# Attention products of a linear-attention and mixture-of-experts kernel in column tiles of 64 queries, with the state update and the zeroing of the output at other places

## The chip, the cores and the metric

The kernel runs on one core of one Trainium2 chip. The metric is the device time of one execution in microseconds (us). Engines are named as the profile names them: PE is TensorE's matmul, PEld its weight load, DVE is VectorE, ACT is ScalarE, POOL is GpSimd, and SP is SyncE, which here only issues transfers (DMAs).

## The reference

Two stages, one after the other. The first is a linear attention with a decaying state, for 4 batches, 8 heads, 768 steps and a head width of 48:

```python
for t in range(S):
    kt, vt, rt = (k[:, :, t], v[:, :, t], r[:, :, t])
    cur = np.einsum('bhd,bhe->bhde', u[None] * kt, vt)
    y[:, :, t] = np.einsum('bhd,bhde->bhe', rt, state + cur)
    state = w[None, :, :, None] * state + np.einsum('bhd,bhe->bhde', kt, vt)
```

The second takes the result as 3072 tokens of 384 numbers and sends each to the two best of 8 experts. A token's noisy logits are `x @ w_gate + log1p(exp(x @ w_noise)) * noise`; the two largest are chosen and weighted by a softmax over the two; an expert is `relu(x @ w1[e]) @ w2[e]` with a hidden width of 1024; the two weighted results are added. All is float32.

## The kernel before, in words

**Attention** goes over 24 tiles i (`NT`): 6 chunks of 128 steps, and in each chunk the 4 batches, so that tile i is chunk `c = i // 4` of batch `b = i % 4`. A tile has 128 queries on the partitions, and its 8 heads stand as 4 pairs `p` with two heads `s` each. Decay is folded into the keys and queries by powers of `w`, so that a chunk needs three products: the scores of keys against queries, masked to the past; the masked scores times the values; and the queries times the state left by the chunk before.

The order of the work is written out by hand, in the loop at L978. Every engine goes through its own instructions in that order, and waits only on semaphores. Iteration i of the loop puts on the engines, one after the other:

- `load(i+3)` (L117): three DMAs from SP for k, r and v of a later tile, in packets of one head's 48 numbers. SP also issues the store of `x` and the loads of expert weights, in the same queue; from tile 8 on, `out` is zeroed there in 16 pieces of 192 rows (L983), since the experts later add into it.
- `trans(i+1)` (L336): keys and queries of the next tile are transposed on PE (L340), and come out of PSUM through ACT (`kT`, L343) and DVE (`rT`, L345).
- `xtrans(i-1)` (L417): the last tile's result transposed on PE (L420), copied by ACT (L422). `zup(i-1)` (L373): the new state, on DVE (`zt`, L381) and ACT (`z` L383, `zb` L385).
- `uterm_b(i+1)`, `prep_k(i+2)`, `uterm_a(i+2)`: the `u` term and decayed keys on POOL (L313 to L322), DVE (L327, and L330 up to tile 8) and ACT (`cv` L333, later).
- `yout(i)` (L388): for each pair one product of the queries with the state (L394, 96 columns wide, from chunk 1 on) and two products of masked scores `AM` with values (L402), all into one PSUM bank `py`. The values are 48 wide, but each product streams them twice, the second time into 48 columns of the bank that nobody reads. Stationary is in both cases a 128x128 block with all 128 queries.
- `xout(i)` (L406): DVE adds the `u` term (L410) and SP stores the result.
- `logits(i-1)` (L425): 3 products with the gate and noise weights (L432); the 16 columns are streamed `LREP` = 6 times side by side, and one copy is read.
- `scores(i+1)` (L348): 8 products with 64 rows each (L352), and `mask(i+1)` (L356): two DVE operations (L360) that write `AM` of the next tile.
- `kvup(i)` (L364): 8 products of keys and values for the next state (L370), 48 columns each, into partitions 0 to 47 and 64 to 111 of the bank `pwarm`. None in the last chunk.

PE makes two passes, each with its own weight load, of every float32 product, so 8 products are x16 in the profile. Between these steps `rstep(us)` (L945) puts pieces of the routing of the tiles 0 to 7, and later 8 to 15, on DVE: each call may spend some us of credit (1.2, 1.1 and 0.3 in a tile), and it holds still for two calls around each of the few PE pieces of the routing.

**Experts** follow. `xT` transposes gathered tokens and splits them into a high and a low part; `p1` makes the hidden layer (L863) and `p2` the output (L897), with three products for each full one. The first products of expert 0, `p1(0, 0)`, begin at about 164 us. The routing of the last 8 tiles goes on beside them, and scatters into `out` follow when the gates are known.

Of the kernel before, what the change touches and what calls it, by code (L numbers as in the profile page):

```python
# [34 lines left out]
NLD = 4  # L35
XT_AT_0 = 4
XT_AT = 4
LREP = 6
NOT = 4

W_LD = {1: (0,), 2: (1, 2), 4: (3,), 5: (4,), 6: (5,), 7: (6,)}
# [5 lines left out]
def kernel(  # L47
# [14 lines left out]
    nc = tc.nc  # L62
    B, H, S, D = r.shape
    N, E = noise.shape
    DM = H * D
# [4 lines left out]
    ND = DM // 128  # L70
    NF = FF // 128
    NT = B * NCH
# [42 lines left out]
    rt, kt, vt = {}, {}, {}  # L115
# [21 lines left out]
    wg = const.tile([128, ND, 2 * E], F32, name="wg")  # L137
# [48 lines left out]
    kT, rT = {}, {}  # L186
# [43 lines left out]
    zrow = const.tile([128, DM], F32, name="zrow")  # L230
# [133 lines left out]
    def kvup(i):  # L364
        c, b = divmod(i, B)
        if c == NCH - 1:
            return
        for p in range(NP):
            for s in range(2):
                nc.tensor.matmul(kvp[s * 64:s * 64 + D, p, :], kd[i % 3][:, 2 * p + s, :D],  # L370
                                 vt[i][:, 2 * p + s, :], start=True, stop=True)
# [16 lines left out]
    def yout(i):  # L388
        c, b = divmod(i, B)
        pyb = psum.tile([128, 512], F32, name="py", tag="py0")  # L390
        py = pyb[:, :DM].rearrange("p (h d) -> p h d", d=D)
        for p in range(NP):
            if c:
                nc.tensor.matmul(py[:, 2 * p:2 * p + 2, :], rT[i][:, p, :], ZB[b][:, p, :],  # L394
                                 start=p == 0, stop=False, skip_group_check=True)
            for s in range(2):


                h = 2 * p + s
                o1 = pyb[:, h * D:(h + 1) * D]  # L400
                o2 = bass.AP(tensor=o1.tensor, offset=o1.offset, ap=[o1.ap[0], [DM - h * D, 2], [1, D]])
                nc.tensor.matmul(o2, AM[i][:, s, p, :], vt[i][:, h, None, :].to_broadcast([128, 2, D]),  # L402
                                 start=not c and h == 0, stop=h == H - 1, skip_group_check=True)
        PY[i] = py

    def xout(i):  # L406
# [8 lines left out]
    XT = {}  # L415
# [9 lines left out]
    def logits(i):  # L425
        g = [i >= a for a, _ in GROUPS].count(True) - 1
        j = i - GROUPS[g][0]
        if j == 0:
            LG[g] = att_pool[0].tile([128, GB, 2 * E], F32, name="lg")
        pl = psum.tile([128, LREP, 2 * E], F32, name="pl", tag="py1")  # L430
        for d in range(ND):
            nc.tensor.matmul(pl, XT[i][:, d, :], wg[:, d, None, :].to_broadcast([128, LREP, 2 * E]),  # L432
                             start=(d == 0), stop=(d == ND - 1))
        nc.scalar.activation(LG[g][:, j, :], pl[:, 0, :], AF.Copy)


# [410 lines left out]
    def p1(e, ci):  # L847
        w_ = sum(tw(t) for t in chunks(e)[ci])
        xh, xl = XH[e, ci]
        wh, wl = W[e][0]  # L850
        wb = w_ // 128 * 128
        hb = moe.tile([128, NF, 2, 3 * 128], F32R, name="hb", bufs=1)
        ht = moe.tile([128, NF, 2, TAIL], F32R, name="ht", bufs=1) if w_ > wb else None
        HH[e, ci] = (hb, ht)
        parts = [(hb[:, :, :, :wb], 0, wb)] + ([(ht, wb, w_)] if w_ > wb else [])
        for f in range(NF):
            fs = slice(f * 128, (f + 1) * 128)
            nph[0] += 1
            ph = (psum.tile([128, WMAX], F32, name="ph", tag="pa", bufs=2) if nph[0] % 3 else
                  psum.tile([128, WMAX], F32, name="ph", tag="kv"))  # L860
            q = [(a, x, d) for d in range(ND) for a, x in ((wh, xh), (wh, xl), (wl, xh))]
            for j, (a, x, d) in enumerate(q):
                nc.tensor.matmul(ph[:, :w_], a[:, d, fs], x[:, d, :w_], start=(j == 0), stop=(j == len(q) - 1))  # L863
            for h_, a, b in parts:
                nc.scalar.activation(h_[:, f, 0, :], ph[:, a:b], AF.Relu)  # L865
            for h_, a, b in parts:
                nc.vector.scalar_tensor_tensor(h_[:, f, 1, :], ph[:, a:b], 0.0, h_[:, f, 0, :].bitcast(F32),  # L867
                                               op0=ALU.max, op1=ALU.subtract)
            yield
# [3 lines left out]
    def p2(e, ci, step=None):  # L873
        hb, ht = HH[e, ci]
        wh, wl = W[e][1]
        offs = {t: 128 * j for j, t in enumerate(chunks(e)[ci])}

        ts = chunks(e)[ci]
        for t in ts if (e, ci) != seq[-1] else ts[-1:] + ts[:-1]:
            n, o = tw(t), offs[t]  # L880
            py = psum.tile([128, DM], F32, name="pym", tag=f"py{np2[0] % 2}")
            np2[0] += 1
            ot = moe.tile([128, DM], F32, name="ot", bufs=NOT)
            OT[e, t] = ot
            hs = slice(o, o + n)
            if n == 64:
                for f in range(NF):
                    nc.tensor.matmul(py, ht[:, f].rearrange("p a b -> p (a b)"), wh[:, f, :], start=(f == 0), stop=(f == NF - 1),  # L888
                                     skip_group_check=True)
                    nc.tensor.matmul(py[:n], ht[:, f, 0, :], wl[:, f, :], start=False, stop=(f == NF - 1),  # L890
                                     skip_group_check=True)
                nc.scalar.activation(ot[:n], py[64:], AF.Copy)
                nc.vector.tensor_add(ot[:n], py[:n], ot[:n])
            else:
                q = [(a, x, f) for f in range(NF) for a, x in ((0, wh), (0, wl), (1, wh))]
                for j, (a, x, f) in enumerate(q):
                    nc.tensor.matmul(py, hb[:, f, a, hs], x[:, f, :], start=(j == 0), stop=(j == len(q) - 1))  # L897
                    if step and j % 8 == 7:
                        step()
                if (e, ci) == seq[-1]:  # L900
                    OT[e, t] = py
                else:
                    nc.scalar.activation(ot, py, AF.Copy)  # L903
            yield t
# [40 lines left out]
    def rstep(us):  # L945

        credit[0] = min(credit[0] + us, 1.6 * us + 0.2)
        while route_q:
            if at_pe[0] > 0:
                at_pe[0] -= 1  # L950
                if at_pe[0] > 0:
                    return
            if credit[0] <= 0:
                return
            try:
                c = next(route_q[0])
            except StopIteration:
                route_q.pop(0)
                continue
            if c == "pe":  # L960
                at_pe[0] = gap[0]
                credit[0] -= 0.3
                return
            credit[0] -= c or 0.2
# [6 lines left out]
    def route_when_done(i):  # L971
        for g, (a, b) in enumerate(GROUPS):
            if b == i + 1:
                if not route_q:
                    at_pe[0] = gap[0]
                route_q.append(route(g))

    for i in range(NT):  # L978
        if i + NLD - 1 < NT and i + NLD - 1 > 2:
            load(i + NLD - 1)  # L980
        if i >= NT - 16:
            q = (i - NT + 16) * 192
            nc.sync.dma_start(out[q:q + 192, :].rearrange("(p two) d -> p two d", two=2),  # L983
                              zrow[:96, None, :].to_broadcast([96, 2, DM]))
        if i + 1 < NT:
            trans(i + 1)
        if i == 0:
            prep_k(0, nc.vector)
            uterm_b(0)
        if i:  # L990
            xtrans(i - 1)
            zup(i - 1)
        if i == I_EARLY:
            while GEARLY - 1 not in routed:
                rstep(1)
            early()
        if i + 1 < NT:
            uterm_b(i + 1)
        if i + 2 < NT:
            prep_k(i + 2)  # L1000
            uterm_a(i + 2)
        for p in W_HI.get(i, ()):
            next(wun[p])
        rstep(STEPS_A)
        if i == 0:
            flag = consts_c()
        if i in (0, 3):
            next(flag)
        yout(i)
        xout(i)  # L1010
        if i:
            logits(i - 1)
            route_when_done(i - 1)
        rstep(STEPS_B)
        if i == NT - 1:
            for _ in xT(0, 0):
                pass
            p1a = p1(0, 0)
        if i + 1 < NT:
            scores(i + 1)  # L1020
            mask(i + 1)
        kvup(i)
        rstep(STEPS_KV)
        for p in W_LO.get(i, ()) + W_LD.get(i, ()):
            next(wun[p])
# [4 lines left out]
    next(wun[6])  # L1030
    NLAG[0] = 3
    for j, _ in enumerate(p1a):
        if j == XT_AT_0:
            for _ in xT(0, 1):
                pass
        rstep(STEPS_P1)
    for t in p2(0, 0, lambda: rstep(STEPS_P2 / 3)):
        hold.append((0, t))
    def routes_done():
# [159 lines left out]
```

## Time and profile before

| | |
|---|---|
| time of 3 runs, median | 651.19 us (649.28 to 652.44) |
| span of the profiled execution | 648.8 us |
| mean granted TensorE clock in it | 0.989 |
| PE busy | 625.8 us (96%) |
| PEld busy | 594.9 us (92%) |
| DVE busy | 345.3 us (53%) |
| ACT busy | 262.5 us (40%) |
| POOL busy | 263.2 us (41%) |
| chain that ended last, PE's share | 69% |

The times are of executions without the profiler; the span is from the first to the last instruction of one profiled execution. Shares over the whole span mix the attention, which ends at about 164 us, with the experts, which have a different mix of work, so each is read by itself. [...]

### The profile page before, as it was taken

The numbers are of one execution on the slowest core, as the hardware profiler recorded it, in microseconds if no ns is written. First come the engines' busy times: TensorE is split into PE (matmuls) and PEld (weight loads), VectorE is DVE, ScalarE is ACT, GpSimd is POOL, SyncE is SP. The second block draws the span as 40 slices with busy tenths as digits, with TensorE's granted clock in tenths as the row PEclk, the third lists the DMA queues.
The fourth block names the chain that finished last, engine by engine and source line by source line (L and its number), as shares of the span: only waits on it lengthen the run. The fifth ranks groups of instructions, "written<-read, shape, count | busy, mean of one in ns | idle before, by whom it ended". The sixth has DMA issues, their size and how long they took to land.

```text
span 648.8 us, 11891 instructions
## 1 busy us (share of the span) xinstructions
PE 625.8 (96%) x4436; PEld 594.9 (92%) x4437; DVE 345.3 (53%) x882; ACT 262.5 (40%) x738; POOL 263.2 (41%) x389
## 2 busy tenths in 40 slices
PE   8999999999998988999999999999999999999993
PEld 5899899998998988999999999999999999999993
DVE  6776988786789654436253444525342543523230
ACT  2557667674324244425242433524243342423210
POOL 7857546562012246415422641443273145315211
PEclk9999999999998989999999999999999999999997
DMA  8999877764033256242441624244252425202100
GB/s 129 213 202 198 192 176 168 170 167 114 14 112 117 63 182 199 82 146 94 134 145 71 189 75 153 70 158 140 75 177 75 153 60 178 81 27 87 37 10 30
DMA packets 111444, 78.87 MB, mean 122 GB/s; under 512 B 86721, under 2 KB 101441, under 8 KB 111378
## 3 DMA queue, kind: packets, MB, share of 16 engines
q1 hardware_dynamic: 101442, 49.19, 30.5%
q0 software_dynamic: 9936, 28.83, 14.1%
q8 instruction: 37, 0.61, 0.4%
q14 instruction: 29, 0.24, 0.1%
HBM read 59.03 MB, written 19.76 MB: 121 GB/s over the span
## 4 chain that ended last, share of the span: by engine, by line
PE 69%; DVE 3%; DMA 1%; ACT 1%; issue 0%; POOL 0%; POOLq 0%
PE ph L863 33%; PE pym L897 30%; PE ptm L838 2%; PE pym L890 2%; PE pym L888 2%; DMA stg<-in_moe_w_dram 1%; DVE xl L840 0%; DVE w1l L287 0%; DVE r_oa L516 0%; PE py L402 0%; ACT hb L865 0%; DVE hb L867 0%; PE pl L432 0%; PE RT L529 0%; DVE w0l L287 0%
## 5 line engine op out<-in xcount | busy, mean ns | idle before, releaser
L897 PE MATMUL pym<-w1h,hb 128*128 128x384 f32 x768 | 204.2, 339 | 0.0
L863 PE MATMUL ph<-xh,w0h 128*128 128x384 f32 (+3 forms) x408 | 142.9, 350 | 4.9 <-ACT xh L839 2.8
L918 POOL DMA_INDIRECT out_dram<-ot,TK x56 | 57.2, 1022 | 220.9 <-DVE ot L914 198.1
L863 PE MATMUL ph<-xl,w0h 128*128 128x384 f32 (+3 forms) x408 | 140.1, 343 | 1.8 <-DVE xl L840 1.8
L897 PEld LDWEIGHTS pym<-w1h,hb 128*128 128x128 f32 x768 | 139.4, 188 | 0.8 <-DVE hb L867 0.2
L863 PE MATMUL ph<-xh,w0l 128*128 128x384 f32 (+3 forms) x408 | 140.0, 343 | 0.0
L897 PE MATMUL pym<-w1l,hb 128*128 128x384 f32 x384 | 129.3, 337 | 0.0
L867 DVE SCALAR_TENSOR_TENSOR hb<-ph,hb 128x384 fp32r<-128x384 f32 (+1 forms) x136 | 72.3, 532 | 106.2 <-ACT ht L865 70.1
L865 ACT ACTIVATE hb<-ph 128x384 fp32r<-128x384 f32 (+1 forms) x136 | 64.2, 473 | 118.3 <-PE ph L863 116.0
L903 ACT ACTIVATE ot<-pym 128x384 f32<-128x384 f32 x45 | 22.1, 492 | 160.0 <-PE pym L897 160.0
L863 PEld LDWEIGHTS ph<-xh,w0h 128*128 128x128 f32 x408 | 77.5, 190 | 8.4 <-ACT xh L839 3.4
L811 POOL DMA_INDIRECT xg<-xd,GR x56 | 54.3, 970 | 75.1 <-DVE f L693 32.7
L863 PEld LDWEIGHTS ph<-xl,w0h 128*128 128x128 f32 x408 | 77.8, 191 | 5.0 <-DVE xl L840 2.5
L863 PEld LDWEIGHTS ph<-xh,w0l 128*128 128x128 f32 x408 | 77.6, 190 | 2.6
L840 DVE TENSOR_TENSOR xl<-ptm,xh 128x384 fp32r<-128x384 f32 (+1 forms) x56 | 29.0, 523 | 81.4 <-ACT xh L839 81.4
L897 PEld LDWEIGHTS pym<-w1l,hb 128*128 128x128 f32 x384 | 72.2, 188 | 0.1
L820 POOL DMA_INDIRECT pv<-out_dram,GA x49 | 55.2, 1127 | 28.8 <-issue 13.7
L402 PE MATMUL py<-vt,am 128*128 128x96 f32 x384 | 58.8, 278 | 1.9 <-DVE am L360 0.8
L402 PEld LDWEIGHTS py<-vt,am 128*128 128x128 f32 x384 | 50.2, 192 | 4.1 <-DVE am L360 3.7
L313 POOL TENSOR_TENSOR kd<-kt,tabk 128x192 f32<-128x192 f32 x46 | 29.0, 652 | 51.6 <-PE pwarm L370 34.8
L360 DVE TENSOR_TENSOR am<-pa,mneg 128x512 int32<-128x512 int32 x48 | 30.7, 681 | 14.3 <-PE pa L352 14.2
L914 DVE SCALAR_TENSOR_TENSOR ot<-ot,GT,pv 128x384 f32<-128x384 f32 (+1 forms) x46 | 27.0, 610 | 11.0 <-ACT ot L903 11.0
(205 smaller groups left out, 864.6 us busy)
## 6 DMA issues: line engine op xcount, KB each, us to landing
stg<-in_moe_w_dram SPq DMA_DIRECT2D x24, 512.0 KB, 4.2
stg<-in_moe_w_dram SPq DMA_DIRECT2D x32, 384.0 KB, 3.4
rd<-in_r_dram SPq DMA_DIRECT2D x24, 192.0 KB, 4.5
vt<-in_v_dram SPq DMA_DIRECT2D x24, 192.0 KB, 4.3
xd<-x SPq DMA_DIRECT2D x24, 192.0 KB, 2.8
out_dram<-zrow SPq DMA_DIRECT2D x16, 288.0 KB, 4.1
kt<-in_k_dram SPq DMA_DIRECT2D x23, 192.0 KB, 3.9
xg<-xd,GR POOLq DMA_INDIRECT x56, 3.1
```

The costliest lines, as they stand in the source:

```text
L313: (eng or nc.gpsimd).tensor_mul(kd[i % 3][:, h, :D], kt[i][:, h], tabk[:, h, :D])
L360: nc.vector.tensor_tensor(am[:, s].bitcast(I32), pa[s].bitcast(I32), mneg.to_broadcast([128, NP, 128]), op=ALU.bitwise_and)
L402: nc.tensor.matmul(o2, AM[i][:, s, p, :], vt[i][:, h, None, :].to_broadcast([128, 2, D]), start=not c and h == 0, stop=h == H - 1, skip_gr ...
L811: nc.gpsimd.indirect_dma_start(out=xg[:n], out_offset=None, in_=xd[:GROUPS[GEARLY - 1][1] * 128] if early_ else xd, in_offset=bass.Indirec ...
L820: nc.gpsimd.indirect_dma_start(out=pv[:n], out_offset=None, in_=out, in_offset=bass.IndirectOffsetOnAxis(ap=GA[:n, e * NJ + t:e * NJ + t + ...
L840: nc.vector.tensor_sub(xl[:, :, o:o + n], pt[:, :, :n], xh[:, :, o:o + n].bitcast(F32))
L863: nc.tensor.matmul(ph[:, :w_], a[:, d, fs], x[:, d, :w_], start=(j == 0), stop=(j == len(q) - 1))
L865: nc.scalar.activation(h_[:, f, 0, :], ph[:, a:b], AF.Relu)
L867: nc.vector.scalar_tensor_tensor(h_[:, f, 1, :], ph[:, a:b], 0.0, h_[:, f, 0, :].bitcast(F32), op0=ALU.max, op1=ALU.subtract)
L897: nc.tensor.matmul(py, hb[:, f, a, hs], x[:, f, :], start=(j == 0), stop=(j == len(q) - 1))
L914: nc.vector.scalar_tensor_tensor(ot[:n], pt[:n], g, PV[e, t][:n], op0=ALU.mult, op1=ALU.add)
L918: st = nc.gpsimd.indirect_dma_start(out=out, out_offset=bass.IndirectOffsetOnAxis(ap=TK[:n, q:q + 1], axis=0), in_=ot[:n], in_offset=None, ...
```

## The change

- `yout`: each product is made in two column tiles of 64 queries (`q`), which go to partitions 0 to 63 and 64 to 127 of `py`. The values are streamed once instead of twice. Each half has its own first product, which clears the sums.
- `logits`: also two column tiles; `LREP` is 4 instead of 6, so 64 columns are streamed instead of 96.
- `kvup(i)` stands ahead of `scores(i+1)` and `mask(i+1)`.
- The 16 pieces of zeroing: 8 in the last 8 tiles, 7 between the pieces of `p1(0, 0)`, and one after it, instead of one in each of the last 16 tiles.

```diff
-LREP = 6
+LREP = 4
@@ yout
+        first = [True, True]
+
+        def acc_mm(o, lhsT, rhs, q, last):
+            qs = slice(q * 64, (q + 1) * 64)
+            nc.tensor.matmul(o[qs], lhsT[:, qs], rhs, start=first[q], stop=last, skip_group_check=True)
+            first[q] = False
+
         for p in range(NP):
             if c:
-                nc.tensor.matmul(py[:, 2 * p:2 * p + 2, :], rT[i][:, p, :], ZB[b][:, p, :],
-                                 start=p == 0, stop=False, skip_group_check=True)
+                for q in range(2):
+                    acc_mm(py[:, 2 * p:2 * p + 2, :], rT[i][:, p, :], ZB[b][:, p, :], q, False)
             for s in range(2):
                 h = 2 * p + s
-                o1 = pyb[:, h * D:(h + 1) * D]
-                o2 = bass.AP(tensor=o1.tensor, offset=o1.offset, ap=[o1.ap[0], [DM - h * D, 2], [1, D]])
-                nc.tensor.matmul(o2, AM[i][:, s, p, :], vt[i][:, h, None, :].to_broadcast([128, 2, D]),
-                                 start=not c and h == 0, stop=h == H - 1, skip_group_check=True)
+                for q in range(2):
+                    acc_mm(py[:, h, :], AM[i][:, s, p, :], vt[i][:, h, :], q, h == H - 1)
@@ logits
         for d in range(ND):
-            nc.tensor.matmul(pl, XT[i][:, d, :], wg[:, d, None, :].to_broadcast([128, LREP, 2 * E]),
-                             start=(d == 0), stop=(d == ND - 1))
+            for q in range(2):
+                qs = slice(q * 64, (q + 1) * 64)
+                nc.tensor.matmul(pl[qs], XT[i][:, d, qs], wg[:, d, None, :].to_broadcast([128, LREP, 2 * E]),
+                                 start=(d == 0), stop=(d == ND - 1), skip_group_check=True)
@@ the loop over tiles
+    def zero_out(j):
+        nc.sync.dma_start(out[j * 192:(j + 1) * 192, :].rearrange("(p two) d -> p two d", two=2),
+                          zrow[:96, None, :].to_broadcast([96, 2, DM]))
+
     for i in range(NT):
...
-        if i >= NT - 16:
-            q = (i - NT + 16) * 192
-            nc.sync.dma_start(out[q:q + 192, :].rearrange("(p two) d -> p two d", two=2),
-                              zrow[:96, None, :].to_broadcast([96, 2, DM]))
+        if i >= NT - 8:
+            zero_out(i - NT + 8)
...
+        kvup(i)
         if i + 1 < NT:
             scores(i + 1)
             mask(i + 1)
-        kvup(i)
...
     for j, _ in enumerate(p1a):
+        zero_out(8 + j)
...
+    zero_out(15)
```

## Rows read from the trace of the kernel before

**Rows 1.** Windows: length, busy us (count) by engine, PEclk, DMA share, GB/s.

```profile
17.95:66.30 48.35, 48.21 (x563) 45.68 (x563) 36.50 (x64) 29.48 (x85) 34.19 (x52) 1.00 1.00 208
66.30:153.36 87.06, 84.20 (x961) 79.21 (x960) 74.52 (x258) 61.70 (x217) 44.62 (x77) 1.00 0.73 165
153.36:163.63 10.27, 9.64 (x88) 8.86 (x86) 4.66 (x12) 4.40 (x17) 4.02 (x4) 1.00 0.50 145
```

**Rows 2.** Windows of tiles 3, 9, 12, 20 and 21; same columns.

```profile
29.16:34.72 5.56, 5.56 (x69) 5.29 (x68) 5.39 (x11) 2.90 (x10) 2.44 (x4) 1.00 0.41 125
...
66.30:73.74 7.44, 6.54 (x76) 5.97 (x74) 7.06 (x23) 4.75 (x18) 5.71 (x10) 1.00 0.84 206
...
86.70:93.50 6.80, 6.66 (x85) 6.28 (x84) 4.65 (x21) 5.10 (x18) 3.67 (x8) 1.00 0.90 193
...
139.25:146.26 7.01, 6.17 (x68) 5.83 (x67) 4.75 (x18) 5.29 (x18) 5.19 (x10) 1.00 0.67 171
146.26:153.36 7.10, 6.53 (x65) 5.97 (x66) 6.57 (x19) 3.80 (x12) 0.00 (x0) 1.00 0.30 75
```

**Rows 3.** Timeline of PE in tile 6: start us, us to last end, line, count.

```profile
48.55 0.39 PE L394 MATMUL py<-zb,rT 128*128 128x96 f32 x2
48.77 0.61 PE L402 MATMUL py<-vt,am 128*128 128x96 f32 x4
49.22 0.39 PE L394 MATMUL py<-zb,rT 128*128 128x96 f32 x2
...
49.89 0.83 PE L432 MATMUL pl<-wg,xT 128*128 128x96 f32 x6
50.66 1.16 PE L352 MATMUL pa<-rT,kT 64*128 64x128 f32 x16
51.75 0.56 PE L370 MATMUL pwarm<-vt,kd 128*48 128x48 f32 x16
52.24 0.66 PE L340 MATMUL pt<-ident,kd 128*128 128x128 f32 x4
...
53.50 0.36 PE L394 MATMUL py<-zb,rT 128*128 128x96 f32 x2
```

**Rows 4.** Lines in tile 6, PE: count, busy us, mean ns of one, idle.

```profile
L402 PE MATMUL py<-vt,am 128*128 128x96 f32 x16 | 2.4, 275 | 0.0
...
L352 PE MATMUL pa<-rT,kT 64*128 64x128 f32 x16 | 1.2, 285 | 0.0
...
L370 PE MATMUL pwarm<-vt,kd 128*48 128x48 f32 x16 | 0.6, 212 | 0.0
```

**Rows 5.** Timeline of DVE from tile 5 to tile 6.

```profile
45.59 1.29 DVE L360 TENSOR_TENSOR am<-pa,mneg 128x512 int32<-128x512 int32 x2 [1.14 <-PE pa L352]
46.79 1.21 DVE L287 TENSOR_TENSOR w0l<-stg,w0h 128x1024 fp32r<-128x1024 f32 x1
...
48.53 0.34 DVE L381 TENSOR_TENSOR zt<-pwarm,z 128x192 f32<-128x192 f32 x1
...
50.09 0.56 DVE L410 TENSOR_TENSOR x<-py,cv 128x384 f32<-128x384 f32 x1
```

**Rows 6.** Timeline of ACT in tile 14.

```profile
100.21 0.49 ACT L422 ACTIVATE xT<-ptx 128x384 f32<-128x384 f32 x1 [0.17 <-PE ptx L420]
101.26 1.01 ACT L383 ACTIVATE z<-zt,w 128x48 f32<-128x48 f32 x4 [0.56 <-DVE zt L381]
...
103.05 1.91 ACT L333 ACTIVATE cv<-vt,c 128x48 f32<-128x48 f32 x8
104.87 0.16 ACT L434 ACTIVATE lg<-pl 128x16 f32<-128x16 f32 x1
```

**Rows 7.** Windows among the experts; columns as in the first group.

```profile
200.00:205.00 5.00, 3.22 (x20) 2.65 (x20) 4.93 (x10) 2.67 (x8) 0.00 (x0) 0.95 0.25 79
205.00:210.00 5.00, 5.00 (x32) 4.80 (x31) 4.18 (x14) 1.23 (x5) 2.25 (x5) 0.71 0.57 197
```

**Rows 8.** DMA issues: count, KB each, median us from issue to landing.

```profile
out_dram<-zrow SPq DMA_DIRECT2D x16, 288.0 KB, 4.1
```

## The prediction

> **What bounds the kernel now.** I read the windows first, stage by stage. The change touches the attention (up to 163.63 us) alone, so only that part of the span can move, apart from what it hands on late. In tiles 1 to 8 PE is busy 48.21 of 48.35 us, DVE 36.50 [rows 1]: PE is the bound. In tiles 9 to 21 PE is busy 84.20 of 87.06 us, but DVE 74.52 as well [rows 1]. Here the reader has to go tile by tile: DVE's load is uneven, because the routing comes in bursts. In nine of the thirteen tiles (9, 10, 11, 13, 15, 17, 18, 19, 21) DVE is busy 5.9 us or more, 7.06 of 7.44 in the first and 6.57 of 7.10 in the last; summed over the nine, 57.3 us in 60.4. The other four (12, 14, 16, 20), 26.7 us together, have less: 4.65 in the first, 4.75 in the last [rows 2]. So PE is the bound in fourteen tiles (the last two too, below), and in the nine DVE stands right behind it.
>
> Then the timeline of PE in a tile without waits gives the parts of its 6.27 us [rows 3]: `yout` 4 groups of 0.67 (48.55 to 49.22), 2.67; logits 0.77; scores 1.09; `kvup` 0.49; transposes up to the next `yout` 1.26. The difference of starts is what counts here, not the busy time, since matmuls overlap.
>
> **The step of one instruction.** A group's length less the mean duration of its last member, over one step fewer than its members, is the step from start to start [rows 3, 4]. L402: (0.61 - 0.275) / 3 = 111 ns. Scores, which use two halves of 64 rows in turn: (1.16 - 0.285) / 15 = 58 ns. `kvup`, which uses two column tiles of 48 in turn, full 128 rows, float32, and is thus what the change makes of the others: (0.56 - 0.212) / 15 = 23 ns. So two column tiles do run beside each other in this kernel. The rest of each group (1.09 - 0.88 and 0.49 - 0.35) is 0.2 and 0.14 us at the switch from one tiling to the next. Now there are three switches in a tile (into scores, into `kvup`, out of it); afterwards also three (into `yout`, from `kvup` into scores, out of scores), since `yout`, logits and `kvup` share one tiling. That is what the new order is worth: without it there would be four or more.
>
> **Part by part, on PE.** A step for 64 columns isn't in the trace. Between 23 ns at 48 columns and 58 ns at 128, both in pairs, a straight line gives 30 ns. The lower bound is 23; the upper is half of today's 111, 56 ns, if half the columns halve the step and nothing runs in pairs. For L394, 96 wide, I take 37 ns: between 30 and 44, which is 96/128 of the scores' 58. `yout` has 16 instructions of L394 and 32 of the masked scores, instead of 8 and 16: 16 x 37 + 32 x 30 = 1.55 us instead of 2.67. Logits have 12 of 64 columns instead of 6: 0.36 us and a little of the switch, instead of 0.77. Together PE saves 1.4 us in a tile and needs 4.85 us (bounds: 2.0 saved with 23 ns everywhere, about 0.1 with 56). Tiles 0 to 3 have no L394, and save 1.1.
>
> **What is late next.** This is where most of the sum is decided; the saving on PE would be over 30 us if nothing else were near.
> Tiles 5 to 8: DVE's own cycle, with PE out of the way, is from the start of the mask to the end of `x`, 45.59 to 50.65, 5.06 us [rows 5]. The mask waits for scores now, 1.14 us; the new place of `kvup` keeps scores from coming as early as they could, and `kvup` itself waits until DVE has read the old state (L381), behind one weight split of 1.21 us [rows 5]; scores and the next mask queue behind it on PE. I take a period of 5.1 us instead of 6.26, that is 3 x 1.16 = 3.5 for tiles 5 to 7, 0.85 for tile 8 (ACT takes over `cv` there), 0.95 for tile 4. Tiles 1 and 2 give 0.7 and 1.0. Tile 3 gives 0.25: DVE is busy 5.39 of 5.56 [rows 2]. That is 7.2 us. The DMA queues are at a share of 1.00 over this stretch [rows 1] and the same bytes would have to come in 41 us, a share of 1.18; loads run three tiles ahead, and I take 1 us off. Sum for tiles 1 to 8: 6.2 us.
> Nine tiles with DVE at 57.3 of 60.4 us: they can go to DVE's time and no lower. With 0.1 us of wait each, 2.1 us.
> Four tiles with little DVE: ACT is next. From `xT` at 100.21 to the end of the logit copy at 105.03 is 4.82 us, of which 0.56 is a wait for DVE [rows 6]; the next `xT` needs PE to transpose after that copy, since both share a PSUM bank, 0.5 us or so. 5.4 to 5.6 a tile, 22.0 instead of 26.7: 4.7 us.
> Tiles 22 and 23, 10.27 us with PE busy 9.64 [rows 1]: PE saves 1.4 in each on paper, but the mask of tile 23 lies open between scores and `yout` already. I take 1.6, and 0.3 for the last logits.
>
> Sum: 6.2 + 2.1 + 4.7 + 1.9 = 14.9 us.
>
> **The edits that I cost at nothing.** Zeroing: 8 of the 16 transfers of 288 KB leave tiles 8 to 15, where the DMA share is below 1 (0.73 over the stretch [rows 1]), and come behind the last attention tile, where `p1(0, 0)` needs weights that are already there. Each takes 4.1 us to land [rows 8], SP's queue holds them one behind another. The scatters into `out` are programmed only behind the next chunk's `p1`. SP's store of the last gates queues behind them; it is read by the gather of expert 0's last chunk, two `p1` and a `p2` later, which is the cover. Without it the store could come one transfer, 4 us, late. The masks come up to 0.36 us later behind `kvup`, but logits are 0.4 shorter.
>
> After 163.63 us nothing is removed or added on PE, so the rest of the span keeps its length.
>
> [...] `kvup`'s pair of instructions takes 46 ns for two loads of 48 columns and two streams of 48 [rows 3, 4], so loads and streams of the same 128 rows lie beside each other. [...]
>
> **Rivals.** (1) Load and stream of a pair follow each other. Weights of 64 columns take half of 111 ns, 56; streams, with `kvup`'s 46 for 48 wide as a ceiling, 46, 92 and 61. Then `yout` is 16 x 102 + 8 x 148 = 2.8 us, logits 6 x 117 = 0.70: a tile as long as now, 651 us. Against it stands `kvup`'s row; for it, only that `kvup` doesn't add several products into the same sums, as `yout` does. 10%.
> (2) Slower: the two tiles don't pair at all in these products, each instruction takes 56 ns for its weights, and L394 takes 96/128 of the pair of scores, 87 ns. `yout` is 32 x 56 + 16 x 87 = 3.2 us, 0.5 more than now. It costs that where PE is the bound (14 tiles, 7 us) and some 0.1 in the nine others: 659 us. The point from which it decides is a mean step of 56 ns over `yout`'s 48 instructions (2.67 us). 10%.
> (3) The clock. [...] 17%.
>
> **How the numbers follow.** The profiled execution has a span of 648.8 us, 2.4 below the median of the runs; with 14.9 off both, 633.9 of span and 636.3 of time. I put 636. Its own range is 628 (23 ns steps, and DVE's waits closing up, 22 us gained) to 642 (44 ns steps, 1 us less in the tiles where PE is bound), and holds 58%. Below it 5%. Rival 3 holds 17%, between 641 and 649; rival 1 10%, 648 to 654; rival 2 10%, 654 to 663. The range from 627 to 651 takes in the forecast, rival 3 and half of rival 1: 82%. A measurement of this kernel can tell about 0.5%, 3.3 us, from no change: faster (below 647.9) 0.77, same 0.12, slower 0.11.
>
> **What the changed profile would show.** L402's group in a quiet tile: x8 with a step near 30 ns, `yout` near 1.6 us; at 50 ns and more, rival 1 or 2. Tiles 5 to 8 about 5.1 us, with PE now idle ahead of L402, released by DVE L360. Tiles 9, 10, 13 and 18 hardly shorter, with DVE busy all through. Tiles 12, 14 and 16 near 5.5 us. PEclk 1.00 up to the experts; rows below 1 there are rival 3. From the first L863 on the same length as now. The forecast is wrong if the steps are right but DVE's chain has waits that I don't see (masks late, loads late), so that tiles 5 to 8 stay above 5.8 us, or if the first experts start later against the last tile.

## The result, and the profile after

| | before | after |
|---|---|---|
| median time | 650.24 us (4 runs, 648.98 to 652.44) | 642.38 us (4 runs, 641.10 to 642.78) |
| ratio | | 0.987, 95% interval 0.9838 to 0.9902 |
| span of the profiled execution | 648.8 us | 641.0 us |
| mean granted clock (share of full speed) | 0.989 | 0.978 |

The gain is 7.9 us; 14.9 were forecast. The same changed kernel was timed twice more, beside the kernel before, on other occasions: 642.01 us (ratio 0.9864, 0.9830 to 0.9898) and 635.30 us (0.9774, 0.9743 to 0.9805). The kernel before stood at 650.26 and 650.50 us there. Much of what follows is about those 7 us between two measurements of one and the same program. Below, "A" is the execution of the result, and "D" the profiled execution of the third occasion, which has a span of 632.9 us.

Windows of A, in the columns of [rows 1]: tiles 1 to 8, 9 to 21, 22 and 23, then by themselves tiles 9, 12, 20, 21 and 8.

```profile
19.18:63.39 44.21, 40.67 (x782) 36.21 (x783) 36.03 (x64) 29.32 (x86) 32.77 (x49) 0.96 1.01 221
63.39:142.89 79.50, 69.92 (x1354) 62.08 (x1351) 74.03 (x257) 60.17 (x217) 46.83 (x78) 0.98 0.75 155
142.89:156.06 13.17, 10.12 (x148) 8.71 (x144) 4.66 (x12) 4.51 (x17) 4.01 (x4) 0.74 0.40 121
...
63.39:70.69 7.30, 6.45 (x107) 5.87 (x105) 6.96 (x22) 4.52 (x18) 6.82 (x12) 0.80 0.89 167
82.98:88.75 5.77, 5.54 (x116) 4.90 (x113) 5.00 (x21) 5.11 (x18) 3.07 (x6) 1.00 0.76 150
130.67:136.38 5.71, 5.14 (x101) 4.45 (x97) 5.18 (x21) 4.71 (x18) 3.39 (x6) 1.00 0.87 203
136.38:142.89 6.51, 5.36 (x100) 4.61 (x97) 6.41 (x19) 4.03 (x13) 0.00 (x0) 1.00 0.32 79
56.27:63.39 7.12, 5.31 (x108) 4.69 (x106) 4.66 (x11) 5.58 (x19) 4.57 (x7) 0.96 0.94 211
```

The same of D: tiles 1 to 8, 9 to 21, 22 and 23, and tile 8.

```profile
18.55:63.24 44.69, 41.02 (x782) 36.42 (x783) 36.00 (x63) 29.18 (x86) 30.01 (x49) 0.96 1.02 222
63.24:142.51 79.27, 68.70 (x1354) 60.77 (x1352) 73.79 (x258) 60.34 (x217) 46.85 (x78) 1.00 0.73 155
142.51:150.44 7.93, 6.80 (x148) 6.07 (x144) 4.66 (x12) 4.40 (x17) 4.32 (x4) 1.00 0.58 173
...
56.52:63.24 6.72, 5.12 (x108) 4.54 (x106) 4.29 (x10) 5.43 (x19) 3.35 (x6) 1.00 0.89 202
```

Against [rows 1] (48.35, 87.06 and 10.27 us) the stretches are, in us:

| | forecast | A | D |
|---|---|---|---|
| start of tile 0, and tile 0 | 0 | +1.2 | +0.6 |
| tiles 1 to 8 | -6.2 | -4.1 | -3.7 |
| tiles 9 to 21 | -6.8 | -7.6 | -7.8 |
| tiles 22, 23 | -1.9 | **+2.9** | -2.3 |
| from the first L868 to the end | 0 | -0.2 | -2.7 |
| span | -14.9 | -7.8 | -15.9 |

So PE is no longer the bound in tiles 9 to 21 as a whole: it is busy 69.92 of 79.50 us, and DVE 74.03. And one row sets A apart from D: tiles 22 and 23, 13.17 us against 7.93. Tiles 5, 6 and 7 of A by themselves:

```profile
40.44:45.40 4.96, 4.96 (x108) 4.54 (x106) 4.20 (x9) 3.86 (x11) 4.83 (x8) 1.00 0.84 193
45.40:51.30 5.90, 5.31 (x107) 4.59 (x105) 5.69 (x9) 3.83 (x11) 5.40 (x8) 1.00 1.07 232
51.30:56.27 4.97, 4.97 (x108) 4.54 (x106) 4.78 (x9) 3.64 (x11) 4.23 (x7) 1.00 0.94 228
```

Timeline of PE in tile 7 of A, the answer to [rows 3].

```profile
51.09 0.39 PE L396 MATMUL py<-zb,rT 128*64 128x96 f32 x4
51.30 0.39 PE L396 MATMUL py<-vt,am 128*64 128x48 f32 x8
51.52 0.35 PE L396 MATMUL py<-zb,rT 128*64 128x96 f32 x4
51.70 0.39 PE L396 MATMUL py<-vt,am 128*64 128x48 f32 x8
...
52.72 0.53 PE L437 MATMUL pl<-wg,xT 128*64 128x64 f32 x12
53.08 0.53 PE L370 MATMUL pwarm<-vt,kd 128*48 128x48 f32 x16
53.54 1.16 PE L352 MATMUL pa<-rT,kT 64*128 64x128 f32 x16
54.63 0.66 PE L340 MATMUL pt<-ident,kd 128*128 128x128 f32 x4
...
56.05 0.39 PE L396 MATMUL py<-zb,rT 128*64 128x96 f32 x4
```

And the means of one instruction there, from the groups by line, as in [rows 4].

```profile
L396 PE MATMUL py<-zb,rT 128*64 128x96 f32 x20 | 1.8, 261 | 0.0
L396 PE MATMUL py<-vt,am 128*64 128x48 f32 x33 | 1.8, 218 | 0.0
```

By the prediction's own method the masked scores step (0.39 - 0.218) / 7 = 25 ns, the queries with the state (0.35 - 0.261) / 3 = 30 ns. In groups as short as four and eight this leaves out much: from the start of one group to the start of the next, eight masked scores take 0.22 us (51.30 to 51.52), 27 ns each, and four queries with the state 0.18 (51.52 to 51.70), 45 ns each; a pair of heads repeats every 0.40 us. Both are far below the 111 ns of one product with 128 queries, and below half of it.

### The profile page after: what moved, and what is told of

Its sections match the earlier page's. It is cut to its first block, busy times and chain, and to the rows that moved or that the text cites. A ratio compares the mean times of both kernels' runs of the same rounds, so it can differ in the third digit from the quotient of the medians.

```text
span 641.0 us, 13269 instructions
## 1 busy us (share of the span) xinstructions
PE 601.5 (94%) x5124; PEld 565.6 (88%) x5125; DVE 344.7 (54%) x882; ACT 260.6 (41%) x738; POOL 266.5 (42%) x389
## 4 chain that ended last, share of the span: by engine, by line
PE 70%; DVE 2%; DMA 1%; ACT 1%; issue 1%; POOL 0%; POOLq 0%; SPq 0%
PE ph L868 32%; PE pym L902 31%; PE ptm L843 3%; PE pym L895 2%; PE pym L893 2%; DMA stg<-in_moe_w_dram 1%; ACT w0h L285 0%; DVE xl L845 0%; PE py L396 0%; DVE hb L872 0%; DVE r_oa L521 0%; DVE ot L921 0%; ACT hb L870 0%; DVE w0l L287 0%; PE pl L437 0%
## 5 line engine op out<-in xcount | busy, mean ns | idle before, releaser
L868 PE MATMUL ph<-xh,w0h 128*128 128x384 f32 (+3 forms) x408 | 142.5, 349 | 5.1 <-ACT xh L844 2.7
L868 PE MATMUL ph<-xl,w0h 128*128 128x384 f32 (+3 forms) x408 | 139.6, 342 | 1.8 <-DVE xl L845 1.8
L868 PE MATMUL ph<-xh,w0l 128*128 128x384 f32 (+3 forms) x408 | 139.5, 342 | 0.0
L816 POOL DMA_INDIRECT xg<-xd,GR x56 | 54.3, 969 | 76.0 <-DVE f L698 35.7
L868 PEld LDWEIGHTS ph<-xh,w0h 128*128 128x128 f32 x408 | 77.2, 189 | 8.8 <-ACT xh L844 3.3
L868 PEld LDWEIGHTS ph<-xl,w0h 128*128 128x128 f32 x408 | 77.2, 189 | 5.0 <-DVE xl L845 2.5
L868 PEld LDWEIGHTS ph<-xh,w0l 128*128 128x128 f32 x408 | 77.2, 189 | 2.6
L825 POOL DMA_INDIRECT pv<-out_dram,GA x49 | 56.2, 1146 | 30.4 <-issue 14.9
L396 PE MATMUL py<-vt,am 128*64 128x48 f32 x768 | 40.0, 231 | 2.2 <-DVE am L360 2.1
L396 PEld LDWEIGHTS py<-vt,am 128*64 128x64 f32 x768 | 34.9, 148 | 4.4 <-DVE am L360 3.5
```

The costliest lines, as they stand in the source:

```text
L396: nc.tensor.matmul(o[qs], lhsT[:, qs], rhs, start=first[q], stop=last, skip_group_check=True)
L816: nc.gpsimd.indirect_dma_start(out=xg[:n], out_offset=None, in_=xd[:GROUPS[GEARLY - 1][1] * 128] if early_ else xd, in_offset=bass.Indirec ...
L825: nc.gpsimd.indirect_dma_start(out=pv[:n], out_offset=None, in_=out, in_offset=bass.IndirectOffsetOnAxis(ap=GA[:n, e * NJ + t:e * NJ + t + ...
```

## The experiments

There were twelve further runs, in three sets of four on three chips; times within a set are compared with each other. The kernel before had 650.26, 650.76 and 650.50 us in the sets. On which chip the result itself was measured is not on record.

### First set: what held A back

**The changed kernel again**, with no edit.

> The changed kernel once more, as the measure of what differs from one execution to the next and as the reference for the other runs of this job. Expected: 641 to 643 us. In its first profile the granted clock fell to 0.5 at 15.1, 62.9 and 148.2 us, and tiles 22 and 23 took 13.2 us instead of the 10.3 of before, with PE's completions arriving 2 to 3 us late. If these come from the work itself, they stand here again at the same places; if they are one execution's, the places move or vanish and tiles 22 and 23 are at about 8 to 9 us.

Measured 642.01 us (639.15 to 644.24). In its trace tiles 22 and 23 take 12.76 us again. So tile 22 of A was no accident of one execution.

**The old order of scores and state update.**

```diff
-        kvup(i)
         if i + 1 < NT:
             scores(i + 1)
             mask(i + 1)
+        kvup(i)
```

> The changed kernel with the scores and the mask of the next tile ahead of the state update again, as in the kernel before. What the prediction says the new order is worth: one tiling switch less in a tile, 0.14 to 0.2 us. If that is right, each tile in which PE is the bound (about ten here) is 0.2 us longer, 2 us together: 644 us. The rival: the order only decides when the mask can start on DVE, and scores that come 0.5 us earlier help the tiles where DVE waits for them: 1 to 2 us faster, 640 us. No difference (within 1 us) if both are hidden.

Measured 642.53 us (641.75 to 644.47), the same as the run beside it. PE in tile 7 of it:

```profile
51.87 0.53 PE L437 MATMUL pl<-wg,xT 128*64 128x64 f32 x12
52.34 1.16 PE L352 MATMUL pa<-rT,kT 64*128 64x128 f32 x16
53.43 0.56 PE L370 MATMUL pwarm<-vt,kd 128*48 128x48 f32 x16
53.92 0.66 PE L340 MATMUL pt<-ident,kd 128*128 128x128 f32 x4
```

Logits now end with a switch (0.47 us to the scores instead of 0.36 to `kvup`), and the tile takes 5.03 us instead of 4.89 in the run beside it. The fourth switch is there and costs 0.14 us, but PE sets the period in few tiles: it is lost in the sum.

**ScalarE's eight copies behind the logit copy.**

```diff
-            for h in range(H):
-                nc.scalar.activation(cv[:, h, :], vt[i][:, h, :], AF.Copy, scale=c8[:, h, :])
+            def late():
+                for h in range(H):
+                    nc.scalar.activation(cv[:, h, :], vt[i][:, h, :], AF.Copy, scale=c8[:, h, :])
+            CVL.append(late)
@@ behind logits(i - 1)
+            while CVL:
+                CVL.pop(0)()
```

> The changed kernel with the eight ACT operations on cv (from tile 9 on) behind the small copy of the logits instead of ahead of it; nothing else. In the profile of the changed kernel PE waited 8.9 us, and its weight loads 11.8, for that copy, since the transposes of the next x go to the same PSUM bank, and DVE's first routing step waited 1.5 us for it in tile 8. Theory A (ACT's order is the new bound in the tiles with little routing, and the cause of the long tile 8): these waits vanish, tile 8 goes from 7.1 to about 5.5 us, tiles 12, 14, 16 and 20 by 0.3 to 0.5 each: 3 to 4 us faster than the changed kernel, 638.5 us. Theory B (DVE's chain is the bound everywhere and the waits for the copy lie beside it): the waits go over into waits for the mask, at most 0.5 us of difference.

Measured 638.46 us (634.71 to 639.49), 3.5 less than the run beside it. ACT in tile 8 of A, then one line of A's waits (total us, times, longest):

```profile
58.98 0.74 ACT L385 ACTIVATE zb<-z 64x192 f32<-64x192 f32 x2
59.73 1.92 ACT L333 ACTIVATE cv<-vt,c 128x48 f32<-128x48 f32 x8
61.55 0.82 ACT L285 ACTIVATE w1h<-stg 128x768 fp32r<-128x768 f32 x1
62.28 0.16 ACT L439 ACTIVATE lg<-pl 128x16 f32<-128x16 f32 x1
...
PEld ptx L423 <- ACT lg L439: 11.8, 12, 2.0
```

And with the copies late, the line numbers two higher:

```profile
58.90 0.73 ACT L387 ACTIVATE zb<-z 64x192 f32<-64x192 f32 x2
59.65 0.85 ACT L285 ACTIVATE w1h<-stg 128x768 fp32r<-128x768 f32 x1
60.41 0.16 ACT L441 ACTIVATE lg<-pl 128x16 f32<-128x16 f32 x1
60.47 1.90 ACT L334 ACTIVATE cv<-vt,c 128x48 f32<-128x48 f32 x8
...
PEld py L398 <- DVE am L362: 11.3, 22, 1.3
```

In A the logits are in PSUM at 58.21, but ACT's copy comes at 62.28, behind `cv` and a weight split, and PE's next transposes (`ptx`) need that bank. With the copies late this wait is gone from the list, and tile 8 takes 5.05 us instead of 6.84 beside it (7.12 in A). Tiles 9 to 21 take 78.7 instead of 79.8. What PE waits for then is the mask: 11.3 us of PEld in all, 3.5 in A. Theory A was right on tile 8 and on the sum, but not on the four light tiles: only tile 14 got shorter (6.33 to 5.82); 12, 16 and 20 got longer (5.77 to 6.30, 4.89 to 5.18, 5.81 to 6.27), and the nine others gave 1.9 us. By the two kept traces the edit is worth 2.9 us (1.8 in tile 8, 1.1 in 9 to 21); another 2.6 between them lie in tile 4, which it doesn't touch.

**Extra products on PE**, without use, in tiles 0, 9 and 23.

```diff
+    def fill(n):
+        for _ in range(n):
+            nc.tensor.matmul(pwarm[:, 192:512], wsrc[:, :128], wsrc[:, :320], start=True, stop=True, skip_group_check=True)
...
+        fill({9: 12, 23: 14}.get(i, 0))
...
+        fill({0: 18}.get(i, 0))
```

> The changed kernel with idle time of PE filled where the granted clock fell: 18 extra products of 128x320 bf16 (0.14 us each at full clock) behind the scores in tile 0, 12 ahead of the transposes of x in tile 9, and 14 there in tile 23, into columns of a bank that nobody reads. Theory C (the gaps let the clock fall, and each fall costs PE 1 to 2 us): the clock stays at 1.00 up to the experts and the kernel is 2 to 4 us faster than the changed kernel, 639 to 640 us. The rival (what is slow under the low clock is not the bound, since DVE, POOL or a late completion is): the clock stays up and the time is the same within 1 us, or longer by the extra products.

Measured 641.02 us (637.87 to 642.62). The extra products are 320 columns wide; in the kernel before, products of that width start 0.147 us apart at a clock of 1.00 (L863, 208.39 to 210.89 us). Granted clock was 1.00 in tiles 1 and 23, which fell to 4.62 and 3.97 us (5.54 and 5.03 beside it), but 0.50 for 3.41 us at 39.71, where there had been no drop. Tile 22 took 7.52 us all the same, so its length doesn't come from the clock. A gain of 1 us within ranges that overlap: not settled.

### Tile 22

The timeline of A, tile 22: PE, then DVE, then POOL.

```profile
144.08 0.39 PE L396 MATMUL py<-vt,am 128*64 128x48 f32 x8
144.30 0.54 PE L437 MATMUL pl<-wg,xT 128*64 128x64 f32 x12
144.76 1.44 PE L352 MATMUL pa<-rT,kT 64*128 64x128 f32 x16
148.22 0.90 PE L423 MATMUL ptx<-ident,x 128*128 128x128 f32 x3 [2.01 <-issue]
...
146.53 0.56 DVE L413 TENSOR_TENSOR x<-py,cv 128x384 f32<-128x384 f32 x1 [2.67 <-ACT w1h L285]
149.48 0.69 DVE L360 TENSOR_TENSOR am<-pa,mneg 128x512 int32<-128x512 int32 x1 [2.39 <-PE ptx L423]
...
143.70 1.17 POOL L816 DMA_INDIRECT xg<-xd,GR  x1 [8.58 <-DVE GR L689]
```

`yout` ends at 144.47 (144.08 + 0.39), but `x`, which reads it, starts at 146.53, 2.06 us later; scores end at 146.20, the mask starts at 149.48. In tile 23 `x` came 0.10 us behind. The releaser that the profile names, L285, is not an input of `x`; the trace has PE's own semaphore event for `yout` at 146.45. These delays are called the lag below. PE itself was held up too: the scores take 1.44 us instead of 1.16, at a clock of 1.00, and 1.44 to 1.53 in all five traces with the lag, 1.16 in all nine without. So it need not be only the news of finished products that is late; the profile models the ends of products, and the trace can't tell. From 148.20 on the clock is 0.50 for 6.83 us. Beside all this run the first four gathers of tokens (L816).

### Second set: the gathers, and the logit part alone

**Four more gathers, at tile 16**, of the changed kernel and of the kernel before.

```diff
+        if i == 16:
+            for t in range(4):
+                xe = moe.tile([128, XW], F32, name="xg", bufs=6)
+                nc.gpsimd.indirect_dma_start(
+                    out=xe, out_offset=None, in_=xd[:1024],
+                    in_offset=bass.IndirectOffsetOnAxis(ap=row[:, t:t + 1], axis=0))
```

> Four further gathers of 128 rows of x (of the first group's tiles) stand on GpSimd in tile 16 of the changed kernel, where no others run; their rows are not used. Theory: gathers under way hold back the news that PE has done its products. Then in tile 16 or 17 x starts 1 to 2 us behind the last value product (tile 22 of the changed kernel: 2.06 us; tile 16 without the gathers: 0.3 us), and so does the mask behind the scores. Rival: it is something else in tile 22. Then x and the mask start within 0.5 us of PE's end, and tile 16 and 17 grow only by what GpSimd's queue costs the next kd, since four gathers take about 5 us of GpSimd: up to 2 us.

> The same four gathers in tile 16 of the kernel before. Theory that it needs the column tiles' rate of instructions on PE: x and the mask start within 0.5 us of PE's end there, as they do in tile 22 of the kernel before. Rival, that the gathers do it by themselves and tile 22 of the kernel before hides it: x starts 1 to 2 us late here too.

One execution each: 635.95 and 649.72 us. The gathers ran at 99.50 to 104.77 us in the first, beside tile 15; its `x` came 0.16 us behind PE, and 0.10 in tile 16. No lag, in either kernel. But tile 22 of the first, with its own four gathers, took 4.46 us and showed no lag either. So this doesn't answer the question; it raises another, why the lag is gone from tile 22.

**Two of the four early gathers later.**

```diff
         xgather(0, 0, True)
-        xgather(0, 1, True)
...
+    xgather(0, 1, True)
     xtrans(NT - 1)
     next(p1a)
```

> The changed kernel with only two of the four early gathers in tile 22, the other two behind tile 23's last step. Theory that the gathers hold back PE's completions: tile 22 falls from 7.3 us to 6 or less, and the time to 640 to 641 us, unless the later gathers meet the first expert product. Rival, that the lag has nothing to do with the gathers: tile 22 stays over 7 us, and 642 us stays.

Measured 634.10 us (632.52 to 637.06). Tile 22 takes 4.46 us, as the theory would have it. It is nevertheless no evidence for it: POOL had nothing ahead of the moved gathers and issued all four at the same distances behind the start of tile 22 as in A, to 0.01 us (0.80, 2.27, 3.54 and 4.79 us), and the next kernel, with all four in place, has 4.46 us too.

**Without the logit part**: three products of 128 queries and `LREP` 6, as before.

> The changed kernel with the logit products of before (one tile of 128 queries, the gate matrix six times). The prediction's own pricing: 0.41 us a tile on PE in the nine or ten tiles that PE sets, nothing where DVE sets it, so 3 to 4 us of the gain gone: 645 to 646 us. Rival: the logit part is hidden and the time is within 1 us of 642. Second rival: the copies of the gate matrix held the clock up, and the time is below 641.

Measured 643.78 us (640.74 to 645.74), 9.7 more than the kernel with split gathers, which stands in for the changed kernel here (that one was not timed in this set, and the gathers ran at the same distances in both); between their profiled spans lie 5.5 (638.9 and 633.4). PE in tile 7:

```profile
53.01 0.39 PE L396 MATMUL py<-vt,am 128*64 128x48 f32 x8
53.32 0.91 PE L435 MATMUL pl<-wg,xT 128*128 128x96 f32 x6
54.16 0.56 PE L370 MATMUL pwarm<-vt,kd 128*48 128x48 f32 x16
54.66 1.16 PE L352 MATMUL pa<-rT,kT 64*128 64x128 f32 x16
```

From the logits to `kvup` 0.84 us, and 0.31 from the last values to the logits (0.21 in the other kernel): the logit part saves 0.6 us a tile, not 0.41, since in the old form it also stands between two switches. By stretches it is worth 1.2 us in tiles 1 to 8, 2.5 in 9 to 21 and 0.7 in 22 and 23. 3 to 4 us was too low; it is worth 4.4 in the trace and more by the medians (the kept trace of this kernel is its fastest execution). The first rival falls with that; so does the second, that the copies of the gate matrix held up the clock, since they came with more time, not less.

### Third set: program or occasion

**The changed kernel a third time.**

> The changed kernel again, beside the next three on one chip, since the runs with split gathers, with gathers in tile 16 and without the logit part were made on another chip than the runs that showed PE's completions late in tile 22. Theory that the late completions belong to the program (four gathers in tile 22): tile 22 takes 7.3 to 8.1 us again, 642 us. Rival, that they belong to the chip or the run and not to the kernel: tile 22 takes 4.5 us as in the three runs of that other chip, and the time is 637 us or less.

Measured 635.30 us (634.19 to 637.59); its profiled execution is D. The timeline of tile 22 in D, as above:

```profile
143.70 0.39 PE L396 MATMUL py<-vt,am 128*64 128x48 f32 x8
143.92 0.53 PE L437 MATMUL pl<-wg,xT 128*64 128x64 f32 x12
144.38 1.16 PE L352 MATMUL pa<-rT,kT 64*128 64x128 f32 x16
146.28 0.55 PE L423 MATMUL ptx<-ident,x 128*128 128x128 f32 x3 [0.73 <-ACT lg L439]
...
144.19 0.56 DVE L413 TENSOR_TENSOR x<-py,cv 128x384 f32<-128x384 f32 x1 [0.72 <-issue]
145.57 1.29 DVE L360 TENSOR_TENSOR am<-pa,mneg 128x512 int32<-128x512 int32 x2 [0.82 <-PE pa L352]
...
143.31 1.17 POOL L816 DMA_INDIRECT xg<-xd,GR  x1 [7.96 <-DVE GR L689]
```

The same program, the gathers at the same place in the tile, and `x` starts 0.10 us behind `yout`, the mask 0.03 behind the scores. So the program alone does not make the lag; it takes something of the occasion as well.

**Both edits together**, the copies late and the gathers split.

> The changed kernel with ScalarE's eight copies behind the logit copy and two of the four early gathers behind tile 23. Theory that the gathers' number in tile 22 matters: 3.5 us below the run with the copies late alone, and by more than that below the changed kernel beside it: 632 to 634 us if that one is at 642. Rival, that tile 22 depends on the chip or run: tile 22 here is as long as in the changed kernel beside it, and the difference is the 3.5 us of the copies alone.

Measured 634.10 us (632.63 to 637.23), 1.2 below the changed kernel beside it, with ranges that overlap. Tile 8 is shorter here too (5.05 us, 6.72 in D), but in the kept trace tile 4 takes 8.49 us (6.00 in D), where POOL waits 4.2 us for the keys of tile 6; that wait was 4.3 us in the changed kernel of the first set and 3.6 in D. That it beats the changed kernel is not shown where the lag is absent.

**The zeroing at its old tiles.**

```diff
-        if i >= NT - 8:
-            zero_out(i - NT + 8)
+        if i >= NT - 16:
+            zero_out(i - NT + 16)
...
-        zero_out(8 + j)
...
-    zero_out(15)
```

> The changed kernel with the zeroing of the output at tiles 8 to 23 again. The prediction put its move at nothing: within 1 us of the changed kernel beside it. Rival: its 288 KB transfers in tiles 8 to 15 delay the loads of k and r, and the time is 1 to 3 us longer.

Measured 635.55 us (632.56 to 637.42), the same. The move costs and brings nothing that shows.

**The copies late in the kernel before**, the same edit as above.

> The kernel before with ScalarE's eight copies behind the logit copy. Theory that this order costs time only since the column tiles shortened PE's part: within 1 us of the kernel before, as PE is busy without a gap in its tiles 5 to 8, 11, 14 to 16 and 19. Rival, that the copies were in the way already: 2 to 4 us less, at tiles 9, 12, 17 and 20.

Measured 651.76 us (649.23 to 653.63), ratio 1.0016 (0.9995 to 1.0038). Tile 8 takes 6.26 us, with PE busy 6.26, instead of 6.34. Here ACT's order is worth something only once PE is out of the way.

## Why the prediction was right or wrong

**Steps and rivals 1 and 2: right, with some luck.** `yout` takes 1.63 us (51.09 to 52.72), 1.55 forecast; logits 0.36 (0.36); a tile of PE 4.96 (4.85). From group to group a masked score takes 27 ns (30 forecast) and a query with the state 45 (37): two misses that nearly cancel, by luck. The first rival had 0.70 us for the twelve instructions of a pair of heads, and 2.8 for `yout`; measured are 0.40 and 1.63. Loads and products lie beside each other here: in the 1.63 us of `yout` PEld and PE are both busy for 1.63 (A).

What no run separates is the narrower stream from the column tiles: values streamed once by products with all 128 queries were not tried.

**The order of `kvup`: right and worthless.** A fourth switch costs 0.14 us a tile; without the new order the time is the same.

**Tiles 1 to 8: mis-sized, by 2.1 to 2.5 us.** Tiles 5 to 7 took 15.8 us in A (16.2 in D), 15.3 forecast: near, but not as worked out. DVE's cycle was to set 5.1 us in each; tiles 5 and 7 take PE's own 4.96, without a gap on PE, and tile 6 takes 5.90, with DVE busy 5.69 (in D 6.32). Tile 8 was to give 0.85 and lost 0.78 (0.38 in D). The prediction saw that ACT takes over `cv` there, and counted ACT's path to the logit copy for the four light tiles, but not in tile 8, where a weight split of 0.82 stands in the path as well. That the copy's place is the cause is shown: with the copies late tile 8 has 5.05 us. So tiles 6 and 8 stayed above 5.8 us, the prediction's sign of being wrong, but tile 8 for ACT's order and not for a wait in DVE's chain. Tile 1 lost another 0.3 to 0.6 at a granted clock of 0.75 in A and 0.69 in D; at 1.00, in the run with extra products, it took 4.62.

**Tiles 9 to 21: right in sum.** The nine tiles where DVE was the rival gave 3.6 us in A (2.1 forecast), the four light ones 4.0 (4.7). DVE is busy 6.41 of 6.51 in tile 21. The nine took 56.8 us, less than the 57.3 that the prediction called their floor: DVE's work in a tile isn't fixed, and 1.7 us of it had moved to the four light tiles (17.2 us busy there before, 18.9 in A). These come to 22.7 us, near the forecast 22.0, but one by one to 5.77, 6.33, 4.89 and 5.71 where 5.4 to 5.6 was said.

**Tiles 22 and 23: the step that failed in A.** The prediction took 1.6 us for them and 0.3 for the last logits; they lost 2.9. In D they give 2.3. What the prediction couldn't read from a trace of the kernel before is the lag; its term for the work itself was good. This term alone is 4.8 of the 7.1 us between the forecast gain of 14.9 and the 7.8 of A's span. In D the whole sum is off by 1.0 us, and the 635.3 us of that occasion are 0.7 from the forecast. That it comes so near is in part luck: tiles 1 to 8 gave 2.5 us less than forecast and the start 0.6 less, while the experts, which were to give nothing, gave 2.7.

**After the first L868: nothing, as said,** within what the traces vary by: 484.9 us in A, 482.5 in D, 485.2 before, with parts at half clock at different places. All traces of changed kernels lie between 482.4 and 487.7 us here, the three of the kernel before between 483.4 and 485.2.

**Rival 3, the clock: small.** The 642.4 us lie in the band, 641 to 649, that the prediction gave to this rival, but no run shows a term of that size for the clock: of the thirteen tiles 9 to 21 one has a drop in A (0.80 in tile 9) and none in D. The drop in tiles 22 and 23 of A comes behind the lag, when PE had been idle for 2 us. What the prediction didn't have is a drop at the start: 0.50 for 6.83 us from 15.1 us in A and from 15.3 in D, over the end of tile 0 and tile 1. Eight of the eleven traces of changed kernels have one there, and one of three of the kernel before. In the changed kernels the first row of the table goes with it (tile 0 ends at 18.0 to 19.2 us with the drop, at 17.6 to 18.1 without, and at 17.95 in the kernel before), and so do the 0.3 to 0.6 us of tile 1.

**Open.** Why the lag came. Five traces show it, that of the result and the four of the first set (tile 22 at 7.3 to 8.1 us); the six of changed kernels in the second and third set don't (3.8 to 4.5 us). It goes with the occasion; whether with the chip or with something that held only then, the runs can't tell. The clock is not its cause (1.00 in tile 22 of the run with extra products, and 7.52 us all the same), and the four gathers alone don't make it (D has them at the same distances). None of the three traces of the kernel before shows it (`x` 0.09 us behind in tile 22), but none was taken in the first set; its time was the same in all of them. Of the 6.7 us between 642.0 and 635.3 the lag explains about 4.8; the rest lies in stretches that vary from trace to trace.

## What to carry to other kernels

A product whose stationary block has 128 columns can be made in two column tiles of 64, each into its own half of the partitions: the instructions double, and here two of them (27 or 45 ns each) cost less than the one they replace (111 ns). When the bound engine is relieved by a fifth, look at once at what its next instruction in the loop needs from the others: here one short copy, queued behind eight that nobody waited for, took back almost 2 us in a tile, and the same edit was worth nothing before. And time a variant beside its parent on the same occasion: one and the same program stood at 642.0 and at 635.3 us here.

## What was not expected of the hardware

- What waits for a product can start 2 to 3 us after the product's end in the profile: 2.06 us for `x` and 3.28 for the mask in tile 22 of A (0.10 and 0.03 in D), at one place of the program, in the traces of two occasions.
- Pairs of column tiles took 27 ns an instruction with 48 moving columns (0.22 us for eight) and 45 with 96 (0.18 for four), each with a weight load of its own.
- Tile 4, in which POOL waits for keys, took between 5.6 and 8.5 us in executions of programs that don't differ there (6.45 in the kernel before).
